# First expert's weights behind v, zero matmuls, five more PSUM banks and an eight-product last unit in an attention + mixture-of-experts kernel

## The chip, the cores and the metric

One core of one Trainium2 chip. The metric is the device time of one execution in microseconds (us), median of several runs. The kernel before takes 1044.17 us (three runs, 1044.15 to 1045.48). Differences are given as ratios with a 95% interval, and in us only where the trace shows where the us are. The engines by their names in the profile: PE (TensorE, matmuls; PEld is its weight load), DVE (VectorE) and ACT (ScalarE) for elementwise work, POOL (GpSimd, here the v casts and the weight transfers) and SP, which issues the k/q/v and output transfers.

## The reference

```python
# q, k, v: [8, 8, 576, 64]; w_gate [512, 8]; w1 [8, 512, 1024]; w2 [8, 1024, 512]
def _attn_ref(q, k, v):
    q_p, k_p = phi(q), phi(k)                      # phi(x) = x + 1 for x > 0, else exp(x)
    kv = einsum('bhsd,bhse->bhde', k_p, v); z = k_p.sum(2)
    return einsum('bhsd,bhde->bhse', q_p, kv) / (einsum('bhsd,bhd->bhs', q_p, z)[..., None] + 1e-6)

def _moe_ref(x, w_gate, w1, w2):                   # x: [4608, 512]
    P = exp(x @ w_gate - max)
    for _ in range(8):                             # row and column normalisation
        P /= P.sum(1, keepdims=True) + 1e-9
        P /= P.sum(0, keepdims=True) + 1e-9
        P *= N / E
    return sum(P[:, e:e+1] * (maximum(x @ w1[e], 0) @ w2[e]) for e in range(8))
```

## The kernel before

A small planner in Python (`_Plan`) decides the order of every instruction. Each task is given an engine (some may go to either of two, and the plan chooses), a guessed duration, a priority and for a transfer a guessed time to landing (`lat`). The planner runs a list schedule (whenever an engine is free, it takes the ready task of best priority) over these guesses and emits the instructions in that order. On the chip each engine works through its order strictly; semaphores, not the plan's clock, decide when. So a wrong guess makes no wrong result, but it can put an instruction that must wait in front of one that could run.

The work is 16 half batches of attention (`att`), then 8 experts of 9 units of 512 tokens: layer 1 (`hq`, 32 matmuls of 512 columns and 8 relus) and layer 2 (`ye`). Expert 0 uses the plain product, the others a seven-product scheme with sums S of h and T of w2 made on the vector engine. Matmul results go to PSUM banks (here four for ye, two for hq, two for attention); a matmul that needs a bank waits until DVE or ACT has copied out (evicted) what stands there. `acc` is the sum over the experts in SBUF.

```python
    def load_w(e, ten, nm, pl, ap, nk, prio, after=0.0, deps=()):
        g = S_.grp(pl)
        def fn(_):
            g["tile"] = wpool.tile([P, nk, DM * F // (nk * P)], FP16, tag=nm, name=nm)
            nc.gpsimd.dma_start(out=g["tile"], in_=AP(tensor=ten.tensor, offset=e * DM * F, ap=ap))
        t = add(("pool", 1.7), fn, acq=[g], prio=prio, lat=9.0, after=after, deps=deps)
        return g, t
    # ... att(b, g): one half batch, n = 2 * b + g
            tin[nm] = fadd(("sp", 1.05), fn, acq=[gr], prio=pr, lat=2.6)     # k, q, v: 576 KB each
    # ... exp and +1 on ACT or DVE, min and max on DVE, v cast on GpSimd (or DVE for n < 2)
        gkv, gz = [S_.grp(p_att), S_.grp(p_att)], S_.grp(p_kvz)              # p_att: two PSUM banks
    # ... two kv, two qt, den, three num, two xt: ten tiles, all from p_att
    w_t = {0: load_w1(0, prio=-300.0) + load_w2(0, prio=-250.0, after=4.0)}  # first thing in the program
    # ... expert 0: copy ye to acc, and when P is ready
                nc.vector.tensor_scalar(out=acc[g][:, tt, :], in0=acc[g][:, tt, :],
                                        scalar1=P_sb[:, gg, 0:1], scalar2=None, op0=ALU.mult)
            tf = add(("dve", 0.35), f_s, deps=[tf, p_done], prio=NG + g - 400.0)
    # ... combos(e): the four T of expert e from its w2
            last = add(("dve", 0.6), f_T, deps=[tw2, t_close, last], acq=..., prio=NG * e - 4.0)
    # ... expert e >= 2 is loaded when the buffers of expert e - 2 are free
```

The softmax here doesn't subtract the row's maximum and nothing guards it: scores larger than these inputs give would overflow.

Of the kernel before, what the change touches and what calls it, by code (L numbers as in the profile page):

```python
# [9 lines left out]
FP32 = mybir.dt.float32  # L10
# [106 lines left out]
def kernel(  # L117
# [61 lines left out]
    def load_w(e, ten, nm, pl, ap, nk, prio, after=0.0, deps=()):  # L179
        g = S_.grp(pl)  # L180

        def fn(_):
            g["tile"] = wpool.tile([P, nk, DM * F // (nk * P)], FP16, tag=nm, name=nm)
            nc.gpsimd.dma_start(out=g["tile"], in_=AP(tensor=ten.tensor, offset=e * DM * F, ap=ap))  # L184
        t = add(("pool", 1.7), fn, acq=[g], prio=prio, lat=9.0, after=after, deps=deps)
        return g, t

    def load_w1(e, **kw):
        return load_w(e, moe_w1, "w1", p_w1, [[F, P], [F * P, NDT], [1, F]], NDT, **kw)

    def load_w2(e, **kw):
        return load_w(e, moe_w2, "w2", p_w2, [[DM, P], [DM * P, NFT], [1, DM]], NFT, **kw)
# [10 lines left out]
    xt_done = {}  # L203

# [5 lines left out]
    def att(b, g):  # L210
        n = 2 * b + g
        pr = n - 100.0
        src = [[NJ * D, P], [2 * S * D, 2], [1, NJ * D]]
# [41 lines left out]
        tvv.append(fadd({"pool": 1.3, "dve": 0.75} if n < 2 else ("pool", 1.3), f_v, deps=[ta, tin["v"]],  # L255
                        use=[gvv, gin["v"]], prio=pr))
        gkv, gz = [S_.grp(p_att), S_.grp(p_att)], S_.grp(p_kvz)

        def f_kv(_):
            for hh in range(2):  # L260
                gkv[hh]["tile"] = aps.tile([P, 2, D + 1], FP32, tag="att", name=f"kv_ps{hh}")
# [60 lines left out]
        for i0, i1 in ((0, 2), (2, 4), (4, 5)):  # L322
            gn = S_.grp(p_att)

            def f_num(_, i0=i0, i1=i1, gn=gn):
                gn["tile"] = aps.tile([P, 2, 2, 2, D], FP32, tag="att", name="num_ps")
# [93 lines left out]
    w_t = {0: load_w1(0, prio=-300.0) + load_w2(0, prio=-250.0, after=4.0)}  # L420

    def f_init(_):
        make_identity(nc, ident)
        nc.gpsimd.dma_start(out=wg_sb, in_=AP(tensor=moe_w_gate.tensor, offset=0,
                                              ap=[[E, P], [E * P, NDT], [1, E]]))
    add(("pool", 1.5), f_init, prio=-290.0)
    for i in range(2):
        nc.vector.memset(vv_t[i][:, :, :, D], 1.0)
        nc.vector.memset(kvz_t[i], 0.0)
    for b in range(B):  # L430
        att(b, 0)
        att(b, 1)
        if b % 2 == 1:
            logits(b // 2)
    p_done = sinkhorn()
# [16 lines left out]
    def layer1(e, g):  # L452
# [10 lines left out]
        for f in range(NFT):  # L463
# [11 lines left out]
            t1 = add(("pe", 0.87), f_hq, deps=[tw1, prev_hq[0]] + xd, acq=[ghq], use=[gw1], prio=ui + 0.1 * f + 0.35)  # L475
# [12 lines left out]
    def unit0(g):  # L488
        e = 0
# [4 lines left out]
        for half in range(2):  # L494
            for tt in range(4):
                def f_y(_, half=half, tt=tt):
                    if half == 0:
                        gy[tt]["tile"] = yps.tile([P, 512], FP32, tag=f"ye{tt}", name=f"ye{tt}")
                    for f in range(4 * half, 4 * half + 4):
                        nc.tensor.matmul(gy[tt]["tile"], lhsT=gh["tile"][:, f, ds(P * tt, P)], rhs=gw2["tile"][:, f, :],  # L500
                                         start=(f == 0), stop=(f == NFT - 1))
                ty[tt] = add(("pe", 0.87), f_y, deps=[tw2, ty[tt]] + th[4 * half:4 * half + 4],
                             acq=[gy[tt]] if half == 0 else [], use=[gw2, gh],
                             prio=g + 0.1 * (4 * half + tt) + 0.3)
        for tt in range(4):
            def f_fin(eng, tt=tt):
                copy(eng, acc[g][:, tt, :], gy[tt]["tile"])

            def f_s(_, tt=tt):
                gg = 4 * g + tt  # L510
                nc.vector.tensor_scalar(out=acc[g][:, tt, :], in0=acc[g][:, tt, :],
                                        scalar1=P_sb[:, gg, 0:1], scalar2=None, op0=ALU.mult)
            tf = add({"act": 0.65, "dve": 0.69}, f_fin, deps=[ty[tt], t_close if g >= NA else None],
                     use=[gy[tt]], prio=g - 400.0)
            tf = add(("dve", 0.35), f_s, deps=[tf, p_done], prio=NG + g - 400.0)
            for dh in range(2):
                fin_prev[(4 * g + tt, dh)] = tf

    def combos(e):
# [3 lines left out]
        for i in range(4):  # L523
# [9 lines left out]
            last = add(("dve", 0.6), f_T, deps=[tw2, t_close, last], acq=[gT] if i == 0 else [], use=[gw2, gT],  # L533
# [3 lines left out]
    def unit(e, g, gT, tT):  # L537
# [18 lines left out]
        def sub(s):  # L556
# [14 lines left out]
            def pm(lhs, rhs, region, first, deps, acq, prio):  # L571
# [9 lines left out]
                return add(("pe", 0.44), f_m, deps=[tw2, tT] + deps, acq=[g_] if acq else [],  # L581
# [76 lines left out]
```

## Time and profile before

| | us |
|---|---|
| span of the profiled run | 1042.2 |
| TensorE (PE) busy | 1003.0 |
| first matmul of layer 1 | 39.67 |
| period of a unit of experts 1 to 7 | 13.02 |

Busy time includes matmuls at half clock. Lines of the timeline: start, length, engine, line, operation, in brackets the idle time before it and what ended it. This is GpSimd's row of the timeline around 210 us (start, length, engine, line, operation, in brackets the idle time before it and what ended it):

```profile
208.68 0.76 POOL L184 DMA_DIRECT2D w<-in_moe_w_dram  x1 [59.48 <-PE hq L470]
212.99 6.25 POOL L184 DMA_DIRECT2D w<-in_moe_w_dram  x1 [3.56 <-PE ye L500]
```

These are the issues of the third expert's w1 and w2. One normally takes 0.75 to 0.9 us; the second took 6.25. Over the same time DVE does the 36 scalings of acc by P, one every 0.40 us; here are the first 30, and the last one ends at 221.91 us:

```profile
206.57 12.19 DVE L511 TENSOR_SCALAR acc<-acc,P_sb 128x512 f32<-128x512 f32 x30
```

### The profile page before, as it was taken

What the parts mean: (1) busy time and instruction counts of PE and PEld (TensorE: products, weight loads), DVE (VectorE), ACT (ScalarE), POOL (GpSimd) and SP (SyncE); (2) the same over time, 40 slices, a digit from 0 to 9 for tenths busy, and PEclk for the clock granted to TensorE, in tenths of its full rate; (3) what the DMA queues carried; (4) which work ended last, traced back from release to release, by engine and by line L of the source; (5) the groups of instructions that cost most, each with busy time, mean ns of one, the idle gap of its engine ahead of it and who ended that gap; (6) DMA issues with size and microseconds to landing.
All of it is one profiled execution on the core that took longest, in us unless ns stands there. A gap on an engine that the chain in (4) does not pass through costs nothing.

```text
span 1042.2 us, 17323 instructions
## 1 busy us (share of the span) xinstructions
PE 1003.0 (96%) x7192; PEld 645.8 (62%) x7192; DVE 719.4 (69%) x1511; ACT 433.3 (42%) x717; POOL 42.2 (4%) x39
## 2 busy tenths in 40 slices
PE   2699999999999999999999999999999999999997
PEld 1455555456666666666666666666666666666664
DVE  4687775896666766676666766676666766666666
ACT  4677774443333333333333333333333333333331
POOL 2112110020000000000000000000000000000000
PEclk9999999999999999999999999999999999999999
DMA  9969510050004000050004000050004000013333
GB/s 272 309 189 271 168 47 2 1 81 1 1 1 66 17 1 1 1 81 2 1 1 66 16 1 2 1 82 1 1 2 66 16 2 1 1 41 81 81 82 82
DMA packets 31968, 55.66 MB, mean 53 GB/s; under 512 B 2704, under 2 KB 10896, under 8 KB 31888
## 3 DMA queue, kind: packets, MB, share of 16 engines
q1 hardware_dynamic: 18816, 37.76, 12.2%
q0 software_dynamic: 13072, 16.79, 10.1%
q8 instruction: 56, 0.92, 0.4%
q14 instruction: 24, 0.20, 0.1%
HBM read 61.88 MB, written 9.44 MB: 68 GB/s over the span
## 4 chain that ended last, share of the span: by engine, by line
PE 86%; issue 6%; DMA 4%; DVE 2%; ACT 0%; SPq 0%; POOL 0%; DVEq 0%; ACTq 0%; POOLq 0%
PE hq L470 44%; PE ye L579 36%; PE ye L500 3%; DMA vin<-in_v_dram 1%; DMA w<-in_moe_w_dram 1%; DMA qin<-in_q_dram 1%; PE kv_ps L265 1%; PE xt_ps L345 1%; PE qt_ps L291 1%; PE num_ps L329 1%; DVE acc L590 0%; DVE xn L334 0%; PE den_ps L306 0%; SPq L220 0%; DVE kvz L198 0%
## 5 line engine op out<-in xcount | busy, mean ns | idle before, releaser
L474 ACT ACTIVATE h<-hq 128x512 f16<-128x512 f32 x576 | 343.8, 597 | 548.5 <-PE hq L470 547.9
L470 PE MATMUL hq<-xT,w 128*128 128x512 f16 x2304 | 556.9, 379 | 0.0
L590 DVE SCALAR_TENSOR_TENSOR acc<-ye,P_sb,acc 128x256 f32<-128x256 f32 x882 | 396.3, 483 | 141.4 <-PE ye L579 141.4
L470 PEld LDWEIGHTS <-w 128*128 128x128 f16 x2304 | 223.2, 98 | 195.1 <-issue 0.3
L579 PEld LDWEIGHTS <-S 128*128 128x128 f16 x2016 | 196.8, 98 | 53.0 <-DVE S L553 3.7
L579 PE MATMUL ye<-T,S 128*128 128x256 f16 x1512 | 196.0, 273 | 2.4 <-DVE S L553 2.4
L579 PEld LDWEIGHTS <-h 128*128 128x128 f16 x1512 | 147.8, 98 | 58.6 <-issue 0.8
L553 DVE TENSOR_TENSOR S<-h 128x1024 f16<-128x1024 f16 x126 | 86.7, 688 | 112.5 <-ACT h L474 112.5
L579 PE MATMUL ye<-w,h 128*128 128x256 f16 x1008 | 130.8, 273 | 0.4 <-ACT h L474 0.4
L500 PE MATMUL ye<-w,h 128*128 128x512 f16 x288 | 69.8, 379 | 0.0
L579 PE MATMUL ye<-T,h 128*128 128x256 f16 x504 | 65.3, 273 | 0.3 <-DVE acc L590 0.2
L579 PE MATMUL ye<-w,S 128*128 128x256 f16 x504 | 65.3, 273 | 0.2 <-DVE S L553 0.2
L184 POOL DMA_DIRECT2D w<-in_moe_w_dram x16 | 19.1, 1193 | 638.8 <-PE hq L470 603.4
L553 DVE TENSOR_TENSOR S<-h,S 128x1024 f16<-128x1024 f16 x63 | 43.1, 684 | 0.0
L553 DVE TENSOR_TENSOR S<-S,h 128x1024 f16<-128x1024 f16 x63 | 42.9, 681 | 0.0
L500 PEld LDWEIGHTS <-h 128*128 128x128 f16 x288 | 26.1, 98 | 25.0
L334 DVE TENSOR_TENSOR xn<-num_ps,rden 128x512 f16<-128x512 f32 (+1 forms) x48 | 26.3, 595 | 2.8 <-PE num_ps L329 2.4
L200 POOL CAST vv<-vin 128x1152 f16<-128x1152 f32 x16 | 21.8, 1363 | 121.1 <-PE kv_ps L265 82.5
L229 ACT ACTIVATE ek<-kin 128x1152 f16<-128x1152 f32 x16 | 18.6, 1161 | 16.8 <-DMA kin<-in_k_dram 12.8
L265 PE MATMUL kv_ps<-vv,tk 64*128 64x130 f16 x288 | 12.3, 228 | 12.9 <-POOL vv L200 12.7
L198 DVE CAST kvz<-kv_ps 64x65 f16<-64x65 f32 x32 | 6.6, 222 | 22.1 <-ACT kvz L196 12.3
L291 PE MATMUL qt_ps<-ident,tq 128*128 128x128 f16 x144 | 14.6, 240 | 6.8 <-DVE kvz L198 4.6
(59 smaller groups left out, 329.5 us busy)
## 6 DMA issues: line engine op xcount, KB each, us to landing
w<-in_moe_w_dram POOLq DMA_DIRECT2D x16, 1024.0 KB, 9.6
kin<-in_k_dram SPq DMA_DIRECT2D x16, 576.0 KB, 5.2
qin<-in_q_dram SPq DMA_DIRECT2D x16, 576.0 KB, 4.9
vin<-in_v_dram SPq DMA_DIRECT2D x16, 576.0 KB, 6.1
out_dram<-acc SPq DMA_DIRECT2D x72, 128.0 KB, 2.4
wg_sb<-in_moe_w_gate_dram POOLq DMA_DIRECT2D x1, 8.0 KB, 15.3
```

Source lines behind the costliest of these rows:

```text
L184: nc.gpsimd.dma_start(out=g["tile"], in_=AP(tensor=ten.tensor, offset=e * DM * F, ap=ap))
L200: nc.gpsimd.tensor_copy(out=dst, in_=src)
L229: nc.scalar.activation(out=ge["tile"], in_=gin[nm]["tile"], func=AF.Exp)
L265: nc.tensor.matmul(gkv[hh]["tile"], lhsT=gt["k"]["tile"][s, j, :, :].rearrange("p r d -> p (r d)"), rhs=gvv["tile"][s, :, j, :], start=(j ...
L291: nc.tensor.transpose(gp["tile"][:, j - j0, :, :].rearrange("p h w -> p (h w)"), gt["q"]["tile"][:, j, :, :].rearrange("p r d -> p (r d)") ...
L334: nc.vector.tensor_tensor(out=gxn["tile"][:, i0:i1], in0=gn["tile"][:, 0:i1 - i0].rearrange("p i r h e -> p i (r h) e"), in1=grd["tile"][: ...
L470: nc.tensor.matmul(ghq["tile"], lhsT=gw1["tile"][:, c, ts(f, P)], rhs=xT[c][:, ds(512 * g, 512)], start=(c == 0), stop=(c == NDT - 1))
L474: nc.scalar.activation(out=gh["tile"][:, f, :], in_=ghq["tile"], func=AF.Relu)
L500: nc.tensor.matmul(gy[tt]["tile"], lhsT=gh["tile"][:, f, ds(P * tt, P)], rhs=gw2["tile"][:, f, :], start=(f == 0), stop=(f == NFT - 1))
L553: nc.vector.tensor_tensor(out=Sx[:, i], in0=a0, in1=a1, op=op)
L579: nc.tensor.matmul(g_["tile"][:, col, :], lhsT=lhs(kk), rhs=rhs(kk), start=(first and kk == 0), stop=(kk == 3), skip_group_check=True)
L590: nc.vector.scalar_tensor_tensor(out=dst, in0=g_["tile"][:, col, :], scalar=P_sb[:, gg, e:e + 1], in1=dst, op0=ALU.mult, op1=ALU.add)
```

## The change

Its intent: the attention of batch 0 should not share the DMA queues with the first expert's 4 MB of weights, PE should be warm and not held up by PSUM banks, and the last unit should not wait for sums S that nothing covers any more. Core of the diff (the merging of `unit0` into `unit_plain` cut):

```diff
-    def load_w(e, ten, nm, pl, ap, nk, prio, after=0.0, deps=()):
+    def load_w(ten, nm, pl, ap, cut, e, prio, parts=1, after=0.0, deps=(), lats=(9.0,)):
...    (each of `parts` DMAs: columns of w1 or row blocks of w2, plan ("pool", 1.1), lat=lats[i])
-    w_t = {0: load_w1(0, prio=-300.0) + load_w2(0, prio=-250.0, after=4.0)}
+    w_t = {0: load_w1(0, prio=-290.0, parts=2, deps=[vcast[0]], lats=(5.0, 7.0))
+           + load_w2(0, prio=-280.0, parts=2, deps=[vcast[1]], lats=(7.0, 9.0))}
+    add(("pool", 0.8), f_wg, prio=-270.0, deps=[w_t[0][3][1]])
+        def ps_home(kind, i):
+            if n < 2 and kind == "kv":
+                return p_hq, hqp, "hq"
+            if n < 2 and kind == "num":
+                return p_ye[i], yps, f"ye{i}"
+            return p_att, aps, "att"
-        tvv.append(fadd({"pool": 1.3, "dve": 0.75} if n < 2 else ("pool", 1.3), f_v, deps=[ta, tin["v"]],
+        tvv.append(fadd(("pool", 1.3), f_v, deps=[ta, tin["v"]],
+    def f_warm(_):
+        nc.tensor.matmul(yw[0], lhsT=warm[:, 0:P], rhs=warm, start=True, stop=True)
+    for i in range(34):
+        twa = add(("pe", 0.3), f_warm, deps=[twa], use=[gyw], prio=900.0, after=1.2 + 0.5 * i)
-            if e == 0:
-                unit0(g)
+            if e == 0 or (e == E - 1 and g == NG - 1):
+                unit_plain(e, g)
```

More of the change, by code (lines that the diff above doesn't have):

```diff
@@ L177, with f_al, fn @@
     p_ye = [S_.pool(1) for _ in range(4)]
-    def load_w(e, ten, nm, pl, ap, nk, prio, after=0.0, deps=()):
+    def load_w(ten, nm, pl, ap, cut, e, prio, parts=1, after=0.0, deps=(), lats=(9.0,)):
         g = S_.grp(pl)
-        def fn(_):
-            g["tile"] = wpool.tile([P, nk, DM * F // (nk * P)], FP16, tag=nm, name=nm)
-            nc.gpsimd.dma_start(out=g["tile"], in_=AP(tensor=ten.tensor, offset=e * DM * F, ap=ap))
-        t = add(("pool", 1.7), fn, acq=[g], prio=prio, lat=9.0, after=after, deps=deps)
-        return g, t
+        ts_ = []
+        def f_al(_):
+            g["tile"] = wpool.tile([P, ap[1][1], ap[2][1]], FP16, tag=nm, name=nm)
+        tal = add(("none", 0.0), f_al, acq=[g], prio=prio, after=after, deps=deps)
+        for i in range(parts):
+            def fn(_, i=i):
+                dst, a, off = g["tile"], [list(x) for x in ap], e * DM * F
+                if parts > 1:
+                    n = a[cut][1] // parts
+                    off += i * n * a[cut][0]
+                    a[cut][1] = n
+                    dst = dst[:, i * n:(i + 1) * n, :] if cut == 1 else dst[:, :, i * n:(i + 1) * n]
+                nc.gpsimd.dma_start(out=dst, in_=AP(tensor=ten.tensor, offset=off, ap=a))
+            ts_.append(add(("pool", 1.1), fn, use=[g], prio=prio, lat=lats[i], deps=[tal]))
+        return g, [ts_[0], ts_[-1]]
     def load_w1(e, **kw):
-        return load_w(e, moe_w1, "w1", p_w1, [[F, P], [F * P, NDT], [1, F]], NDT, **kw)
+        return load_w(moe_w1, "w1", p_w1, [[F, P], [F * P, NDT], [1, F]], 2, e, **kw)
     def load_w2(e, **kw):
-        return load_w(e, moe_w2, "w2", p_w2, [[DM, P], [DM * P, NFT], [1, DM]], NFT, **kw)
+        return load_w(moe_w2, "w2", p_w2, [[DM, P], [DM * P, NFT], [1, DM]], 1, e, **kw)
     def copy(e, dst, src):
@@ L203 @@
     xt_done = {}
+    vcast = {}
     def fadd(*a, **kw):
@@ L254, in f_v @@
             copy(e, gvv["tile"][:, :, :, 0:D], gin["v"]["tile"])
-        tvv.append(fadd({"pool": 1.3, "dve": 0.75} if n < 2 else ("pool", 1.3), f_v, deps=[ta, tin["v"]],
+        tvv.append(fadd(("pool", 1.3), f_v, deps=[ta, tin["v"]],
                         use=[gvv, gin["v"]], prio=pr))
-        gkv, gz = [S_.grp(p_att), S_.grp(p_att)], S_.grp(p_kvz)
+        vcast[n] = tvv[0]
+        hkv = ps_home("kv", 0)
+        gkv, gz = [S_.grp(hkv[0]), S_.grp(hkv[0])], S_.grp(p_kvz)
         def f_kv(_):
             for hh in range(2):
-                gkv[hh]["tile"] = aps.tile([P, 2, D + 1], FP32, tag="att", name=f"kv_ps{hh}")
+                gkv[hh]["tile"] = hkv[1].tile([P, 2, D + 1], FP32, tag=hkv[2], name=f"kv_ps{hh}")
             for j in range(NJ):
@@ L322, in att, with f_num @@
         for i0, i1 in ((0, 2), (2, 4), (4, 5)):
-            gn = S_.grp(p_att)
-            def f_num(_, i0=i0, i1=i1, gn=gn):
-                gn["tile"] = aps.tile([P, 2, 2, 2, D], FP32, tag="att", name="num_ps")
+            hn = ps_home("num", i0 // 2)
+            gn = S_.grp(hn[0])
+            def f_num(_, i0=i0, i1=i1, gn=gn, hn=hn):
+                gn["tile"] = hn[1].tile([P, 2, 2, 2, D], FP32, tag=hn[2], name="num_ps")
                 for i in range(i0, i1):
@@ L419, with f_wg @@
     nc.vector.memset(ones_t, 1.0)
-    w_t = {0: load_w1(0, prio=-300.0) + load_w2(0, prio=-250.0, after=4.0)}
+    warm = const.tile([P, 512], FP16, tag="warm", name="warm")
+    nc.vector.memset(warm, 0.0)
     def f_init(_):
         make_identity(nc, ident)
+    def f_wg(_):
         nc.gpsimd.dma_start(out=wg_sb, in_=AP(tensor=moe_w_gate.tensor, offset=0,
@@ L426, with f_wa @@
     add(("pool", 1.5), f_init, prio=-290.0)
+    def f_warm(_):
+        nc.tensor.matmul(yw[0], lhsT=warm[:, 0:P], rhs=warm, start=True, stop=True)
+    gyw = S_.grp(p_ye[3])
+    yw = []
+    def f_wa(_):
+        yw.append(yps.tile([P, 512], FP32, tag="ye3", name="yw"))
+    twa = add(("none", 0.0), f_wa, acq=[gyw], prio=-300.0)
+    for i in range(34):
+        twa = add(("pe", 0.3), f_warm, deps=[twa], use=[gyw], prio=900.0, after=1.2 + 0.5 * i)
     for i in range(2):
@@ L474, in f_rl @@
                 nc.scalar.activation(out=gh["tile"][:, f, :], in_=ghq["tile"], func=AF.Relu)
-            t1 = add(("pe", 0.87), f_hq, deps=[tw1, prev_hq[0]] + xd, acq=[ghq], use=[gw1], prio=ui + 0.1 * f + 0.35)
+            t1 = add(("pe", 0.87), f_hq, deps=[tw1[f // 4], prev_hq[0]] + xd, acq=[ghq], use=[gw1], prio=ui + 0.1 * f + 0.35)
             prev_hq[0] = t1
@@ L486, in out_dma, with unit_plain @@
         add(("sp", 1.0), f_o, deps=deps, prio=0.0)
-    def unit0(g):
-        e = 0
+    def unit_plain(e, g):
         gw1, tw1, gw2, tw2 = w_t[e]
@@ L501, in f_y, with f_fin, f_s @@
                                          start=(f == 0), stop=(f == NFT - 1))
-                ty[tt] = add(("pe", 0.87), f_y, deps=[tw2, ty[tt]] + th[4 * half:4 * half + 4],
+                ty[tt] = add(("pe", 0.87), f_y, deps=[tw2[half], ty[tt]] + th[4 * half:4 * half + 4],
                              acq=[gy[tt]] if half == 0 else [], use=[gw2, gh],
-                             prio=g + 0.1 * (4 * half + tt) + 0.3)
+                             prio=e * NG + g + 0.1 * (4 * half + tt) + 0.3)
         for tt in range(4):
-            def f_fin(eng, tt=tt):
-                copy(eng, acc[g][:, tt, :], gy[tt]["tile"])
-            def f_s(_, tt=tt):
-                gg = 4 * g + tt
+            gg = 4 * g + tt
+            def f_fin(eng, tt=tt, gg=gg):
+                if e == 0:
+                    copy(eng, acc[g][:, tt, :], gy[tt]["tile"])
+                else:
+                    nc.vector.scalar_tensor_tensor(out=acc[g][:, tt, :], in0=gy[tt]["tile"],
+                                                   scalar=P_sb[:, gg, e:e + 1], in1=acc[g][:, tt, :],
+                                                   op0=ALU.mult, op1=ALU.add)
+            def f_s(_, tt=tt, gg=gg):
                 nc.vector.tensor_scalar(out=acc[g][:, tt, :], in0=acc[g][:, tt, :],
                                         scalar1=P_sb[:, gg, 0:1], scalar2=None, op0=ALU.mult)
-            tf = add({"act": 0.65, "dve": 0.69}, f_fin, deps=[ty[tt], t_close if g >= NA else None],
-                     use=[gy[tt]], prio=g - 400.0)
-            tf = add(("dve", 0.35), f_s, deps=[tf, p_done], prio=NG + g - 400.0)
-            for dh in range(2):
-                fin_prev[(4 * g + tt, dh)] = tf
+            if e == 0:
+                tf = add({"act": 0.65, "dve": 0.69}, f_fin, deps=[ty[tt], t_close if g >= NA else None],
+                         use=[gy[tt]], prio=g - 400.0)
+                tf = add(("dve", 0.35), f_s, deps=[tf, p_done], prio=NG + g - 400.0)
+                for dh in range(2):
+                    fin_prev[(gg, dh)] = tf
+            else:
+                tf = add(("dve", 0.75), f_fin, deps=[ty[tt], p_done, fin_prev[(gg, 0)], fin_prev[(gg, 1)]],
+                         use=[gy[tt]], prio=e * NG + g - 400.0)
+                out_dma(g, tt, [tf])
     def combos(e):
@@ L532, in f_T @@
                 nc.vector.tensor_tensor(out=T[:, i], in0=a0, in1=a1, op=op)
-            last = add(("dve", 0.6), f_T, deps=[tw2, t_close, last], acq=[gT] if i == 0 else [], use=[gw2, gT],
+            last = add(("dve", 0.6), f_T, deps=tw2 + [t_close, last], acq=[gT] if i == 0 else [], use=[gw2, gT],
                        prio=NG * e - 4.0)
@@ L580, in f_m @@
                                          start=(first and kk == 0), stop=(kk == 3), skip_group_check=True)
-                return add(("pe", 0.44), f_m, deps=[tw2, tT] + deps, acq=[g_] if acq else [],
+                return add(("pe", 0.44), f_m, deps=tw2 + [tT] + deps, acq=[g_] if acq else [],
                            use=[gw2, gT, gh, gS, g_], prio=ui + 0.3 + prio + 0.02 * s)
@@ L618 @@
         if e >= 2:
-            w_t[e] = load_w1(e, prio=float(e), deps=[w_t[e - 1][1]]) + load_w2(e, prio=float(e), deps=[w_t[e - 1][3]])
+            w_t[e] = load_w1(e, prio=float(e), deps=w_t[e - 1][1][1:]) + load_w2(e, prio=float(e), deps=w_t[e - 1][3][1:])
         if e > 0:
```

## The prediction

> **What bounds the kernel now.** I read the page first, its row of slices:
>
> ```profile
> PE   2699999999999999999999999999999999999997
> ...
> PEclk9999999999999999999999999999999999999999
> DMA  9969510050004000050004000050004000013333
> ```
>
> One slice is 26 us. TensorE (PE) is full from the third slice to the last but one. Only the first two slices, where the DMA row shows 9, and the last one have room. I then took the windows view, whose columns are stretch, length, busy time of PE, PEld, DVE, ACT and POOL with counts, granted clock, DMA share, GB/s:
>
> ```profile
> 10.00:15.00 5.00, 1.16 (x18) 0.89 (x17) 0.04 (x1) 0.00 (x0) 1.15 (x1) 1.00 1.12 291
> 35.00:40.00 5.00, 3.48 (x26) 2.75 (x26) 4.32 (x9) 3.73 (x5) 0.00 (x0) 1.00 1.05 390
> 40.00:45.00 5.00, 5.00 (x50) 2.60 (x49) 2.37 (x5) 3.04 (x9) 1.15 (x1) 1.00 0.76 218
> 45.00:50.00 5.00, 3.05 (x26) 1.81 (x25) 4.24 (x10) 3.40 (x5) 0.00 (x0) 1.00 0.81 236
> 220.00:230.00 10.00, 8.61 (x61) 5.63 (x59) 8.81 (x20) 2.90 (x6) 0.00 (x0) 1.00 0.72 104
> 1028.57:1036.50 7.93, 6.09 (x49) 4.10 (x46) 7.01 (x15) 0.60 (x1) 0.00 (x0) 1.00 0.23 52
> 1036.50:1042.20 5.70, 0.01 (x1) 0.00 (x0) 0.53 (x2) 0.00 (x0) 0.00 (x0) 0.83 0.67 156
> ```
>
> PE idles 1042.2 - 1003.0 = 39.2 us. By stretch: 26.65 before 40 us (40 less the eight busy figures there, 13.35), 1.95 in 40 to 50, 1.7 from 50 to 220, 1.39 in 220 to 230, 1.84 in the last unit and 5.69 after the last matmul. Between 230 and 1028 us it is dense: the chain repeats every 13.02 us per unit, which is 32 matmuls of 512 columns and 56 of 256 without a gap. The change leaves that stretch alone, so it can win only at the two ends.
>
> What holds up the first 40 us stands in the chain of waits, cut to the start:
>
> ```profile
> 3.46 15.24 DMA vin<-in_v_dram
> ...
> 20.38 12.49 DMA qin<-in_q_dram
> ...
> 32.90 0.76 DVE tq L235
> 33.66 0.03 issue
> 33.69 0.19 DVE rden L312
> ...
> 39.88 1.04 PE hq L470 x4
> ```
>
> A v load takes 15.2 us and then a q load 12.5. After them the reciprocal of the second half batch (rden) comes late only because DVE has the q cast of a later half batch ahead of it in its order. Layer 1 (hq) cannot start before batch 0, two half batches, is done: 39.67 us in the timeline. The waits of the first 40 us name the beginning:
>
> ```profile
> POOL vv L200 <- DMA vin<-in_v_dram: 15.9, 3, 7.2
> PE kv_ps L265 <- POOL vv L200: 12.7, 1, 12.7
> ```
>
> **What the Trainium skill says.** "DMA: Bandwidth & Descriptors", section SWDGE vs HWDGE vs iDMA: software-made and hardware-made descriptors feed different queues inside each engine, served round-robin, and a cast must be issued by GpSimd. The packet records agree: from 18 to 20 us the weight queue moved 181 packets and the k/q/v queue 182. A 576 KB load landed every 1.5 us alone (30 to 38 us) and every 2.96 us beside w2 (18 to 27 us). "TensorE: Matmul & The Clock Gate", Part 1: a PE left idle about 3.4 us falls to half clock. The PEclk row does not show it (1.00 throughout), but the work does:
>
> ```profile
> 12.66 1.16 PE L265 MATMUL kv_ps<-vv,tk 64*128 64x130 f16 x18 [12.66 <-POOL vv L200]
> ...
> 51.80 0.69 PE L265 MATMUL kv_ps<-vv,tk 64*128 64x130 f16 x18
> ```
>
> The same page, section Architectural detail: DVE and ACT are strictly first in, first out; rden behind a foreign q cast agrees. "PSUM — Partial Sum Buffer", Specifications: eight banks per partition. The kernel has assigned them all: four ye, two hq, two for attention. The six others are empty in the first 39 us, while ten tiles of every half batch take turns on two.
>
> **The change part by part.**
>
> *Weights behind v.* In before the weight issues start at 1.24 and 3.42 us; w1's packets landed 5.4 to 14.2 us, those of w_gate to 17.5, w2's 16.5 to 28.7. The first six loads landed at 4.0, 5.8, 10.6, 14.2, 15.9 and 18.0 us. The two behind q0 have most of w1's packets beside them. Without weights, at 1.5 us each, they become about 4.0, 5.6, 7.1, 8.6, 10.1 and 11.6. The first v cast starts 0.8 us after landing and takes 1.15, so kv runs at about 9.0 instead of 12.66, and the sixth load is in 6.4 us sooner. GpSimd issues w1 behind that first cast, at 9.0. In before 3.5 to 4 us went by from the issue to the first packets, so about 12.5 here. Halving w1 by columns turns 512 packets of 2 KB into 1024 of 1 KB, like w2's, of which 1024 took 12.2 us. Hence halves of 6 us: w1 at 18.5 and 24.5, w2 at 30.5 and 36.5. The later k/q/v loads now share the queue: k2 13, q2 16, v2 19, k3 22, q3 25, v3 28. This does not make DMA traffic less; it moves the attention of batch 0 ahead of the weights.
>
> *Free banks.* For the first two half batches kv goes to hq banks and num to ye banks. That takes five of ten tiles off the two attention banks. In the timeline the second kv matmul ran at 27.75, although its v cast ended at 19.90: 7.8 us lost to banks and orders of engines. With 1.15 for the cast from v1's landing at 11.6 plus 0.8, kv1 can run at 13.5. From its kv (27.75) to its last xT copy (39.25) before needed 11.5 us, of which the rden wait on q3 (landed 31.9) is a few. I take 9 to 11: batch 0 is done at 22.5 to 24.5 if its DVE steps stand only behind loads of half batch 2 (19 us), and at 27 if behind q3 (25). I choose 24.5 for the first hq. w1's first half is there at 18.5. Its second serves hq 5 to 8, from 28 us; w2 serves ye, 8 x 0.86 = 6.9 us of hq plus attention later, 32 us and on. Both just suffice.
>
> *Gain at the front.* 39.67 - 24.5 = 15.2 us. Off that: before had already done nine more transposes by then (0.5 us). Its half batches up to the sixth had nearly all been loaded, whereas in after PE will meet its orders with loads still late (v3 at 28, w2 at 36.5, the plan counts on earlier). I charge 4 us for such stalls, against the 1.95 us in 40 to 50 that before pays. Net: 15.2 - 0.5 - (4 - 1.95) = about 12.5 us.
>
> *Zero matmuls.* 34 of 512 columns: 34 x 0.216 = 7.3 us warm, 14.5 at half clock, all planned within the first 18 us, where PE has 26.65 us of idling. They buy warm attention matmuls: kv 1.16 becomes 0.69, nine or ten transposes 1.3 become about 0.7. That is 1 to 2 us on the chain of batch 0, part of which comes back as a zero matmul standing in front of a ready one (0.2 to 0.4 each). It is inside the 9 to 11 above; I add nothing.
>
> *Last unit.* Seven products cost 56 x 0.109 = 6.1 us, eight (32 matmuls of 512 columns x 0.216) 6.9: +0.8. In before PE ran from the last unit's first product at 1028.41 to 1036.50, 8.1 us, of which 2.0 are waits on the S sums of DVE:
>
> ```profile
> 1032.21 1.05 PE L579 MATMUL ye<-T,S 128*128 128x256 f16 x8 [1.18 <-DVE S L553]
> ```
>
> Those go; one wait for the last relu (0.6) may stay. PE ends 0.6 to 1.2 us sooner. The end behind it is bound by eight issues on SP:
>
> ```profile
> 1034.57 4.96 SPq L485 DMA_DIRECT2D out_dram<-acc  x8
> ```
>
> They cost 0.62 each and end 3.0 us after PE. With tiles finishing every 0.86 us and a 512-wide eviction of about 0.75, the first issue comes about 1.8 before PE's end and the last ends 3.2 after. So 0.2 goes back: gain 0.7 us.
>
> Sum: 12.5 + 0.7 = 13.2 us off 1044.17, so 1031.
>
> **The rivals.** *The orders eat it.* The program's orders come from a plan that counts a load at 1.05 us; on the chip it is 1.5 to 3. For it: the 12.5 us q load of the chain. Against: fewer banks to wait for puts batch 0 further ahead in the orders. If rden of the second half batch stands behind q3 again, hq starts at 27 to 30 and the gain is 7 to 9: 1035 to 1037. *Late weights become the bound.* w_gate comes last, 512 packets of 16 B that took 4.4 us even in before, and the first logits could hold PE some us; so could w2. That gives 2 to 4 us back: about 1034. *Everything runs to schedule.* hq starts at 21, no extra stalls: the gain is 18 to 19 and the result 1025. More is hardly possible: two half batches need their six loads (11.6) and then the chain of the second. *DMA total as the bound*: to 40 us before had loaded 18 tiles and all weights; that is time PE spends well if batch 0 comes first, so I don't believe in no gain at all.
>
> **Range and chances.** Front gain from 6 to 18 us with the tail's 0.7 gives 1025 to 1038. Over 2% means below 1023.3, or 21 us: nearly the whole 26.65 plus 1.95, though the first loads alone forbid 9 of it: 4%. Slower by 2% would need a new wait in the dense part, which the change does not touch: 1%.
>
> **What would show each step.** The first vv cast at about 7.9 and kv at 9.0 us; the second kv near 13.5; w1's halves landing near 18 and 24; the first hq of w near 24.5; PE idle before 40 us down from 26.65 to 12 to 16, the zero matmuls not counted as work; kv x18 near 0.7 in the first 15 us. At the end no S wait in the last unit, and PE ending within 6 us of the span's end. It is wrong if hq starts after 31, if PE shows new waits of over 5 us between 25 and 60 us, or if the 13.02 us rhythm changes.

## More of the kernel before

The scaling of expert 0 by P comes late, since the routing P is ready only when all attention is done.

## The result, and the profile after

The changed kernel takes 1047.66 us (median of four, 1046.31 to 1048.04) beside 1044.80 for the one before: ratio 1.0025, interval 1.0008 to 1.0042. A ratio is the mean time of one kernel's fast runs over that of the other's of the same rounds, so not quite the ratio of the medians that I quote. I had said 1031 and a range of 1025 to 1038.

The profiled run has a span of 1044.5 us, 2.3 more than before. Where they come from is read by following the same matmul through both traces:

| matmul of layer 1 | before, us | after, us | difference |
|---|---|---|---|
| first | 39.7 | 31.4 | -8.2 |
| 17th | 44.6 | 43.0 | -1.5 |
| 289th (first of expert 1) | 208.2 | 206.2 | -2.0 |
| 353rd | 234.2 | 238.0 | +3.9 |
| 2001st | 906.0 | 909.9 | +3.9 |
| end of the span | 1042.2 | 1044.5 | +2.3 |

So the front won 2.0 us, 5.9 were lost between 206 and 238 us, and the end won 1.6. From 238 us on the difference stays at 3.9: the 13.02 us rhythm is untouched. Up to the 289th matmul a row of this table counts layer 1 alone, and the two kernels put different pieces of attention between its matmuls. So I also counted all of PE's work done by a given time, every matmul at its full-clock time (0.216 us for 512 columns, by the trace before), zero matmuls left out: the kernel after leads by 3.2 us at 40 and at 50 us and by 1.8 at 200 us. So of the 8.2 us by which layer 1 starts sooner 3.2 are left at 40 us.

**The front.** The windows view of the kernel after (columns as in the prediction):

```profile
10.00:15.00 5.00, 5.00 (x58) 3.50 (x59) 4.85 (x11) 4.40 (x6) 3.96 (x5) 0.67 1.07 376
35.00:40.00 5.00, 1.12 (x9) 0.56 (x7) 1.29 (x3) 0.97 (x1) 0.70 (x1) 1.00 1.19 328
40.00:45.00 5.00, 4.27 (x20) 2.14 (x20) 1.83 (x4) 4.27 (x7) 0.00 (x0) 0.66 1.04 387
```

At 10 to 15 us PE is full (zero matmuls and half clock included), where before it did 1.16 us. But at 35 to 40 it does 1.12 us instead of 3.48, and all other engines starve as well while the DMA share is 1.19. The chain of waits says on what:

```profile
3.73 9.21 DMA vin<-in_v_dram
...
14.17 11.50 DMA vin<-in_v_dram
...
27.77 11.23 DMA qin<-in_q_dram
39.01 0.02 issue
39.03 1.16 ACT eq L247
40.19 0.49 ACT h L512
40.69 0.04 issue
40.73 1.87 PE hq L508 x4
```

It is the same figure as before, further on. Layer 1 has begun, and its second relu (h) stands on ACT behind the exponential of a q that lands only at 38.1 us. The timeline of ACT shows both places where that happens:

```profile
28.64 1.16 ACT L247 ACTIVATE eq<-qin 128x1152 f16<-128x1152 f32 x1 [2.56 <-DMA qin<-in_q_dram]
29.71 0.62 ACT L206 COPY xT<-xt_ps 128x576 f16<-128x576 f16 x1
...
39.03 1.16 ACT L247 ACTIVATE eq<-qin 128x1152 f16<-128x1152 f32 x1 [5.07 <-DMA qin<-in_q_dram]
40.10 1.06 ACT L512 ACTIVATE h<-hq 128x512 f16<-128x512 f32 x2
```

The last xT copy of batch 0, which frees layer 1, waits from 26.6 to 29.7 behind load 12 (q of the fourth half batch, called q3, its last packet at 27.3); two relus wait until 40.1 behind load 16 (q4, 38.1). The waits of PE that follow are 3.5 and 4.6 us:

```profile
30.38 1.13 PE L285 MATMUL kv_ps<-vv,tk 64*128 64x130 f16 x17 [3.46 <-ACT xT L206]
40.73 1.87 PE L508 MATMUL hq<-xT,w 128*128 128x512 f16 x4 [4.61 <-ACT h L512]
```

Behind each of them matmuls run at half clock (granted 0.62 in 30 to 35 us, 0.66 in 40 to 45).

**The zero matmuls** all ran, but in this run the first 13 did not warm PE:

```profile
1.33 5.51 PE L453 MATMUL yw<-warm 128*128 128x512 f16 x13 [1.33 <-DVE warm L442]
9.93 1.16 PE L285 MATMUL kv_ps<-vv,tk 64*128 64x130 f16 x18 [3.09 <-POOL vv L210]
```

Thirteen took 0.42 us each throughout, and the first kv behind them 1.16, as cold as before. The second kv, at 14.87 us, took 0.69.

**The middle.** GpSimd's and DVE's rows of the timeline after:

```profile
202.85 13.95 DVE L554 TENSOR_SCALAR acc<-acc,P_sb 128x512 f32<-128x512 f32 x35
206.69 11.29 POOL L194 DMA_DIRECT2D w<-in_moe_w_dram  x2 [60.39 <-PE hq L508]
```

```profile
230.41 0.69 DVE L580 TENSOR_TENSOR T<-w 128x1024 f16<-128x1024 f16 x1 [7.05 <-DMA w<-in_moe_w_dram]
231.02 1.65 DVE L638 SCALAR_TENSOR_TENSOR acc<-ye,P_sb,acc 128x256 f32<-128x256 f32 x4
232.33 1.87 PE L627 MATMUL ye<-T,h 128*128 128x256 f16 x8 [6.03 <-DVE acc L638]
```

The first issue alone took 10.41 us, until 217.1, when the row of 35 scalings (202.85 to 216.80) had ended. w2 landed at 230 us. DVE stood 7.05 us before T of the third expert, which is not needed before that expert starts (its first layer-1 matmul is at 329 us). Evictions of layer 2 stood behind it, and PE behind them; two rows of the windows view, the second at a granted clock of 0.74:

```profile
220.00:230.00 10.00, 6.31 (x43) 3.98 (x41) 3.36 (x7) 2.39 (x4) 0.00 (x0) 0.92 1.09 187
230.00:240.00 10.00, 7.67 (x42) 4.65 (x42) 7.07 (x15) 2.39 (x4) 0.00 (x0) 0.74 0.00 0
```

Before, the same 220 to 230 us had 8.61 busy and 230 to 240 had 10.00. The 5.9 us are about the sum: 6.0 of wait, 1.4 of half clock in the twelve matmuls behind it (1.87 + 1.62 us, where the trace shows 1.04 + 1.03 at full clock), less the 1.4 that the kernel before idles there.

**The end.** The last unit's layer 2 and the output issues, timeline after:

```profile
1034.84 3.83 PE L537 MATMUL ye<-w,h 128*128 128x512 f16 x16
...
1036.90 4.95 SPq L523 DMA_DIRECT2D out_dram<-acc  x8
```

No wait for S is left. PE ends at 1038.69, 1.7 us sooner against the lag of 3.9; the issues end 3.2 us behind PE, as the prediction worked out (before: 3.0).

### The profile page after: what moved, and what is told of

Read it like the earlier page. It is cut to its first block, busy times and chain, and to the rows that moved or that the text cites. A ratio compares the mean times of both kernels' runs of the same rounds, so it can differ in the third digit from the quotient of the medians.

```text
span 1044.5 us, 17330 instructions
## 1 busy us (share of the span) xinstructions
PE 1013.9 (97%) x7202; PEld 646.2 (62%) x7202; DVE 713.3 (68%) x1495; ACT 435.8 (42%) x720; POOL 46.9 (4%) x41
## 4 chain that ended last, share of the span: by engine, by line
PE 85%; issue 7%; DMA 4%; DVE 2%; POOL 1%; ACT 0%; SPq 0%; POOLq 0%; DVEq 0%; ACTq 0%
PE hq L508 43%; PE ye L627 36%; PE ye L537 4%; DMA vin<-in_v_dram 2%; DMA w<-in_moe_w_dram 1%; DMA qin<-in_q_dram 1%; PE kv_ps L285 1%; PE xt_ps L366 1%; PE num_ps L350 0%; PE qt_ps L311 0%; POOL w L194 0%; DVE kvz L208 0%; SPq L238 0%; DVE tk L260 0%; POOL vv L210 0%
## 5 line engine op out<-in xcount | busy, mean ns | idle before, releaser
L638 DVE SCALAR_TENSOR_TENSOR acc<-ye,P_sb,acc 128x256 f32<-128x256 f32 x868 | 390.6, 483 | 141.0 <-PE ye L627 140.9
L627 PEld LDWEIGHTS <-S 128*128 128x128 f16 x1984 | 194.1, 98 | 48.9
L627 PE MATMUL ye<-T,S 128*128 128x256 f16 x1488 | 192.8, 273 | 0.0
L627 PE MATMUL ye<-w,h 128*128 128x256 f16 x992 | 128.6, 273 | 0.0
L537 PE MATMUL ye<-w,h 128*128 128x512 f16 x320 | 77.6, 379 | 0.0
L194 POOL DMA_DIRECT2D w<-in_moe_w_dram x18 | 24.9, 1387 | 640.4 <-PE hq L508 609.5
L247 ACT ACTIVATE eq<-qin 128x1152 f16<-128x1152 f32 x16 | 18.6, 1162 | 8.7 <-DMA qin<-in_q_dram 8.3
L206 ACT COPY acc<-ye 128x512 f32<-128x512 f32 x26 | 15.2, 585 | 9.3 <-PE ye L537 8.9
```

The source lines that it names most:

```text
L194: nc.gpsimd.dma_start(out=dst, in_=AP(tensor=ten.tensor, offset=off, ap=a))
L206: nc.scalar.copy(out=dst, in_=src)
L247: nc.scalar.activation(out=ge["tile"], in_=gin[nm]["tile"], func=AF.Exp)
L537: nc.tensor.matmul(gy[tt]["tile"], lhsT=gh["tile"][:, f, ds(P * tt, P)], rhs=gw2["tile"][:, f, :], start=(f == 0), stop=(f == NFT - 1))
L627: nc.tensor.matmul(g_["tile"][:, col, :], lhsT=lhs(kk), rhs=rhs(kk), start=(first and kk == 0), stop=(kk == 3), skip_group_check=True)
L638: nc.vector.scalar_tensor_tensor(out=dst, in0=g_["tile"][:, col, :], scalar=P_sb[:, gg, e:e + 1], in1=dst, op0=ALU.mult, op1=ALU.add)
```

## The experiments

Fifteen kernels, in four groups (e, f, g with f6, h), four or five runs of each; every group ran on another chip. Each ratio is to the kernel before in the same rounds on the same chip (seven to nine runs), so a comparison across groups, such as g4 with f1 or h1 with g4, is one of ratios.

| run | what | median us | ratio (95%) |
|---|---|---|---|
| e1_tlate | after, T later | 1039.41 | 0.9947 (0.9934 to 0.9959) |
| e2_scale_act | after, scalings on ACT | 1039.11 | 0.9945 (0.9932 to 0.9959) |
| e3_b_tlate | before, T later | 1044.52 | 0.9996 (0.9983 to 1.0008) |
| e4_b_eight | before, eight products | 1043.17 | 0.9984 (0.9971 to 0.9996) |
| f1_truelat | e1, true landings in the plan | 1032.77 | 0.9884 (0.9869 to 0.9900) |
| f2_now2 | e1, first w2 not read | 1032.25 | 0.9879 (0.9865 to 0.9892) |
| f4_nowarm | e1, no zero matmuls | 1039.34 | 0.9948 (0.9935 to 0.9960) |
| f5_nobanks | e1, two banks | 1043.86 | 0.9990 (0.9977 to 1.0002) |
| f6_wearly | e1, weights at the start | 1038.11 | 0.9940 (0.9926 to 0.9953) |
| g1_b_truelat | e3, true landings | 1035.81 | 0.9914 (0.9900 to 0.9927) |
| g3_w1late | f1, second expert later | 1032.04 | 0.9882 (0.9868 to 0.9895) |
| g4_nowarm | f1, no zero matmuls | 1031.22 | 0.9872 (0.9859 to 0.9886) |
| h1_wearly_true | g4, weights at the start | 1035.35 | 0.9915 (0.9900 to 0.9929) |
| h2_truelat_only | after, true landings | 1034.08 | 0.9897 (0.9883 to 0.9912) |
| h3_nobanks | g4, two banks | 1032.41 | 0.9888 (0.9871 to 0.9904) |

### The middle: T, scalings and descriptors

My theory after the traces: the 5.9 us in the middle are T in DVE's order, waiting for weights whose descriptors GpSimd could not write while DVE ran its scalings. The rival: DVE's backlog itself holds PE, T is an onlooker.

**e1_tlate.**
```diff
-            last = add(("dve", 0.6), f_T, deps=tw2 + [t_close, last], ...
+            last = add(("dve", 0.6), f_T, deps=tw2 + [t_close, last, hq_at[(e - 1, 5)] if e >= 2 else None], ...
```
(`hq_at[(e, g)]` is the last layer-1 task of a unit.)

> The changed kernel, with one thing more: the four DVE sums T that the third expert needs from its second-layer weights (and those of the later experts) are tied in the plan to layer 1 of a late unit of the expert before, so that they stand some 60 us later in DVE's order. Theory (the loss after 206 us is DVE, in order, standing 7.05 us before a T whose weights came late, though nobody needs that T for another 100 us): the 6.0 us PE wait near 226 to 232 us and the cold matmuls behind it go; the changed kernel was 2.0 us ahead of the one before at the end of the first expert and fell to 3.9 behind, so 5.9 us come back: 1047.4 - 5.9 = about 1041.5, ratio to the kernel before 0.997. Rival (DVE's burst of 36 scalings itself makes PE wait, T is an onlooker): the wait stays or turns up under another name, time stays within 1.5 us of 1047.

It gave 8 us. The wait is gone; the windows view of this run in the stretch where before had 8.61 and after 6.31:

```profile
220.00:230.00 10.00, 10.00 (x70) 6.58 (x68) 7.09 (x15) 3.07 (x6) 0.00 (x0) 1.00 1.10 186
```

Yet its weight issue took 10.41 us as well. So the late landing does no harm by itself; T's place in the order makes it a stall. It gained more than the 5.9 us I expected, 7.4 us between the two profiled runs: 5.9 for the stall, and 1.6 because it now passes this stretch faster than the kernel before, whose 1.39 us of idling there are gone too.

**e2_scale_act.**
```diff
-                nc.vector.tensor_scalar(out=acc[g][:, tt, :], in0=acc[g][:, tt, :],
-                                        scalar1=P_sb[:, gg, 0:1], scalar2=None, op0=ALU.mult)
+                nc.scalar.activation(out=acc[g][:, tt, :], in_=acc[g][:, tt, :], func=AF.Copy, scale=P_sb[:, gg, 0:1])
-            tf = add(("dve", 0.35), f_s, ...
+            tf = add(("act", 0.62), f_s, ...
```

> The changed kernel with the 36 scalings of acc by P moved from DVE to ACT (36 x about 0.6 us, planned there). Theory (those 512-wide SBUF to SBUF DVE operations keep GpSimd from writing the descriptors of the third expert's weights: issue of 10.4 us): the two weight issues near 205 us take 0.7 to 0.9 us each, w2's packets end 8 to 12 us sooner than 230 us, T does not wait and PE's 6.0 us wait goes: about 1041.5 to 1043. Rival (the issue is long because of GpSimd's own wait or of the DMA queue): the issues stay at 6 to 10 us, time stays.

The issues without the burst on DVE, GpSimd's timeline of this run:

```profile
208.11 0.75 POOL L194 DMA_DIRECT2D w<-in_moe_w_dram  x1 [60.36 <-PE hq L508]
212.64 0.89 POOL L194 DMA_DIRECT2D w<-in_moe_w_dram  x1 [3.77 <-PE ye L537]
```

T stays where the change has it and no longer waits; the time is that of e1. Both links are shown: the DVE scalings stretch the issue, T's place turns that into PE time. The Trainium skill has the first link ("SBUF — State Buffer", section SBUF: two separate sides): a DVE operation in a two-port mode locks GpSimd out, so that it "cannot write the descriptors". That these scalings run in such a mode no run here shows directly; the issue times with and without them are what is shown. I had not read it for this change, because the change adds no such operation.

**e3_b_tlate** (the same edit on the kernel before):

> The kernel before with the same later T. Theory: it has the same trap, but only 1.2 us of it (its w1 issue slipped through in 0.76 us), so it gains 0.5 to 1.5 us: ratio 0.9985 to 0.9995; the front and the end of the change are then worth e1 against e3, 2.5 to 3.5 us. Rival (T late costs something in the dense stretch): ratio over 1.000.

Nothing measurable (0.9996). Before has the trap, but its first issue slipped in between two scalings (0.76 us), so DVE waited only 1.2 us before T. PE's idling there (1.39 us) is mostly another wait, 1.2 us for an S that stands behind the last six scalings, and e3 keeps it. A change that moved this region by only 2 us turned DVE's 1.2 us before T into 7.

**e4_b_eight** (`unit_plain` for the last unit of the kernel before, nothing else):

> The kernel before with the last unit in eight products and nothing else of the change. From the traces (6.4 us more lag at the last layer-1 matmul would be the reordered unit; at the end of the span the lag fell from 3.9 to 2.3): the part alone is worth 1.6 us, ratio 0.9985. My prediction had 0.7 (ratio 0.9993). Rival (the SP issues of the output bound the end and nothing is won): ratio 1.000.

0.9984, 1.6 us, as the trace said (the profiled run is 0.6 behind at the 2001st layer-1 matmul and 0.9 ahead at the end). Predicted were 0.7; the interval, 0.4 to 3.0 us, does not exclude that, the traces put it at 1.5 to 1.6.

### The front: orders or bytes

**f1_truelat**, on e1:
```diff
-            tin[nm] = fadd(("sp", 1.05), fn, acq=[gr], prio=pr, lat=2.6)
+            slow = 2 < n < 5 or (n == 2 and nm != "k")
+            tin[nm] = fadd(("sp", 2.95 if slow else 1.5), fn, acq=[gr], prio=pr, lat=3.2)
-    ... lats=(5.0, 7.0)) ... lats=(7.0, 9.0))
+    ... lats=(9.6, 14.5)) ... lats=(17.3, 21.7))
```

> The later-T kernel (1039.41 us, ratio 0.9947), its plan fed with the landings that the changed kernel's trace shows: 1.5 us per k/q/v load, 2.95 for the eight loads beside the weights, 9.6 to 21.7 us for the weight halves of the first expert. Nothing else changes; only the orders of the engines do. Theory A (orders: PE's 3.2 and 4.4 us waits come from ACT standing before loads 15 and 16, which the plan thought landed): those two waits go, PE does 3 to 8 us more work by 45 us, the time falls to 1032 to 1037, ratio 0.988 to 0.993. Theory B (DMA total: batch 1 cannot be done before loads up to the twelfth, 27 us, and w2 up to 37 have landed, in whatever order): the waits only move, time 1038 to 1041, ratio 0.994 to 0.997.

Theory A held: the bytes are the same, the first, second and so on to the sixteenth load land within 0.3 us of where they did in the kernel after, and 6.6 us are gone. But the plan orders the loads and chooses engines too. In the kernel after, v3 went before q3 and two v before q4; here q3 is the eleventh load (24.2 us, there 27.3) and q4 the fourteenth (32.9, there 38.1), the very two that ACT stood behind. ACT ran 709 instructions against 720, DVE 1506 against 1495. So "orders" means the order of instructions, the order of loads and the choice of engine together; no run splits them. The windows view, against 1.12 in 35 to 40 us above:

```profile
25.00:30.00 5.00, 4.98 (x33) 2.30 (x31) 2.74 (x7) 3.25 (x5) 1.15 (x1) 0.66 1.13 294
30.00:35.00 5.00, 5.00 (x40) 2.84 (x38) 4.34 (x10) 3.98 (x6) 0.00 (x0) 1.00 1.14 297
35.00:40.00 5.00, 5.00 (x54) 2.79 (x53) 4.04 (x11) 1.93 (x4) 2.17 (x2) 1.00 1.06 364
```

and its timeline:

```profile
24.98 3.53 PE L510 MATMUL hq<-xT,w 128*128 128x512 f16 x8
```

Layer 1 starts at 25.0 us; I had predicted 24.5.

**f2_now2** (zeros for the first expert's w2, 2 MB less to read; its result is wrong by 35%):

> Wrong on purpose: the later-T kernel with zeros in place of the first expert's second-layer weights, so that 2 MB less are read in the first 40 us and the orders stay (two DVE memsets of about 0.6 us come in). Theory B (DMA total): loads 12 to 16 land 3 to 6 us sooner and all of it reaches PE, ratio 0.989 to 0.991. Theory A (orders): the waits for loads 15 and 16 shrink by the same landings, so this run alone does not tell A from B; but if it gains under 2 us (ratio over 0.993), DMA traffic is not the bound at all.

The sixteenth load landed at 32.4 instead of 38, and 7.1 us were gained. As expected in advance, this alone does not tell orders from bytes: a stale order gets better when its loads come sooner (q4 lands here at 32.4, in f1 at 32.9). Together with f1 it says that the front was limited by the mismatch of the two, and could be mended from either side.

**g1_b_truelat** (the kernel before with T later and its own landings in its plan: per k/q/v load 1.5 to 4.8 us, w1 12.7, w2 23.2):

> The kernel before (weights at the start, no zero matmuls, two banks, seven products), with the later T and with its plan fed with its own landings (v0 10.6 us, k1 14.2, v1 18.0, w1 14.2, w2 28.7). Theory (the change's own front parts need true orders to pay, and true orders alone do part of it): 2 to 5 us faster than before, ratio 0.995 to 0.998, first hq near 34 to 38. Rival 1 (the plan's false landings were the whole trouble, the weights' place does not matter): 7 us or more, ratio under 0.9935. Rival 2 (in before the two banks and v's landing bind, orders do not): ratio over 0.9985.

0.9914, 9 us, first layer-1 matmul at 28.5: Rival 1 by its number. (The later T alone, e3, gave nothing measurable.) Without any part of the change, true landings in the plan alone start layer 1 sooner (28.5) than the change does with false ones (31.4). In the kernel before, as in the change, false landings were the larger trouble.

### The parts of the front

**f6_wearly** (e1 with whole weights at the start and the old figures):

> The later-T kernel (ratio 0.9947) with the weights of the first expert whole and at the start again, as before the change, plan figures of before; banks, zero matmuls and eight products stay. Theory (loading behind v is what lets batch 0 run early, worth 1 to 3 us under the stale plan): ratio 0.9955 to 0.9975, first kv at 12.7 us. Rival (the place of the weights is neutral, DMA moves the same in 37 us): ratio 0.9940 to 0.9953.

0.9940 against 0.9947: neutral. Under false landings, loading behind v brings nothing.

**h1_wearly_true** (the same question with true landings, against g4):

> As the kernel with true landings and without zero matmuls (1031.22 us, ratio 0.9872), but the first expert's weights whole and at the start, the plan fed with the landings of the kernel before. If the weights' place is neutral (DMA moves the same bytes by 37 us): ratio 0.986 to 0.9885. If loading behind v is worth the 3 to 4 us by which v0 lands earlier: ratio 0.9895 to 0.992.

0.9915 against 0.9872, intervals apart: 4 us. That it is the early landing that pays is not shown: counted in PE work as above, h1 is only 0.7 us behind g4 at 60 us (9.7 against 10.4 ahead of the kernel before), and 3.1 at 80 us (5.9 against 9.0). Most of the difference comes from what the two plans do between 60 and 80 us, long after the first expert's weights are in.

**f5_nobanks** (`n < 2` to `n < 0` in `ps_home`, on e1) and **h3_nobanks** (the same on g4):

> The later-T kernel with kv and num of the first two half batches back on the two attention banks. Theory (the bank share of the front's 3.5 us is real but batch 0 then waits for loads anyway): 0 to 2 us slower, ratio 0.9947 to 0.9966. Rival (banks are what lets batch 0 run ahead): 3 us or more slower, ratio over 0.9975, hq after 35 us.

> As the kernel with true landings and without zero matmuls (ratio 0.9872), with kv and num of the first two half batches on the two attention banks again. Under the stale plan the banks were worth 4.5 us. If that was mostly the order that the plan made of them: 0 to 1.5 us here, ratio 0.987 to 0.9887. If the banks themselves hold batch 0 up: 3 us or more, ratio over 0.990.

4.5 us under false landings (0.9990), where ACT's orders now wait 11.9 us in all for q loads and hq for xT 5.7. With true landings 0.9888 against 0.9872, with overlapping intervals: 1.7 us, not told from nothing. The banks' worth was mostly what order the plan made of them.

**f4_nowarm** (`range(34)` to `range(0)` on e1) and **g4_nowarm** (the same on f1):

> The later-T kernel without the 34 zero matmuls. My prediction gave them 1 to 2 us inside the chain of batch 0; the landings after 25 us, which bind later, would hide that. Theory (hidden): kv and transposes of the first 15 us are cold again (1.16 us), hq starts within 1 us of 31.2, ratio 0.994 to 0.996. Rival (the clock matters): 2 us or more slower, ratio over 0.9965.

> The kernel with true landings without the 34 zero matmuls. There hq starts at 25.0 us straight behind batch 0, so a colder chain is not hidden by a late load any more. If the clock is worth the 1 to 2 us of my prediction: ratio 0.9895 to 0.9905, hq at 26 to 27. If DVE, not PE, paces batch 0 (as its chain of waits shows): ratio 0.988 to 0.989, hq at 25.

Without the zero matmuls the time is the same in e1 (0.9948) and no worse in f1 (0.9872 against 0.9884, in different rounds). In the profiled run of f1 they did warm PE (17 zero matmuls in 5.43 us, first kv 0.69), in g4 layer 1 starts 1.5 us later. In PE work f1 is 2.8 us ahead of g4 at 40 us, and 0.4 behind at 240: what they bring early is gone later. They buy nothing in the whole time.

**g3_w1late** (`after=60.0`, `after=70.0` to 100 and 110 for the second expert, on f1):

> The kernel with true landings (1032.77 us, ratio 0.9884), the second expert's weights asked for at 100 and 110 us of the plan in place of 60 and 70, so that they do not share the queue with k/q/v between 48 and 78 us. If those transfers cause the loss there (its lead over before fell from 14 to 9 us of PE work between 60 and 80 us), 2 to 5 us more: ratio 0.984 to 0.987. If the in-order DVE chain of attention causes it whatever the loads do: ratio 0.987 to 0.990.

0.9882, no difference from f1: the second expert's loads are not the main thing that makes f1 lose lead behind 60 us (in PE work 14.0 us at 60 us and 9.6 at 80; g3 has 14.2 and 11.1). The chain of waits there runs through DVE's attention steps in their order; I did not test that further.

**h2_truelat_only** (after, with true landings and T where the change has it):

> The changed kernel with true landings in its plan and nothing else (T stays early in DVE's order, zero matmuls stay). If the stall near 226 us belongs to T's place alone: it stays, and the gain is the front's 6.6 us of 1047.4: about 1041, ratio 0.996 to 0.998. If the shifted front moves the third expert's weight issues off the DVE burst: no stall over 2 us and 1033 to 1035, ratio 0.989 to 0.991.

0.9897, 1034 us: my first theory there fell. The stall did not come back (T waited 1.6 us): in this run the first weight issue slipped in, the second took 6.25, as in before:

```profile
200.78 0.75 POOL L194 DMA_DIRECT2D w<-in_moe_w_dram  x1 [58.60 <-PE hq L509]
205.09 6.25 POOL L194 DMA_DIRECT2D w<-in_moe_w_dram  x1 [3.56 <-PE ye L538]
```

T's early place is needed for the stall, but the first issue being shut out is needed too, and that hangs on where the issue falls in the burst. I did not try to steer that, but the traces agree on it. In all 16 that have the scalings on DVE, an issue that began 0.12 or 0.13 us after the start of a scaling got in (ten of them, 0.75 or 0.76 us, the next scaling 0.7 instead of 0.48), and one that began 0.24 to 0.27 us after it was shut out (ten second issues, six first ones). All that were shut out ended 0.3 to 0.5 us after the row of scalings, when DVE had turned to evictions that read PSUM.

The fastest right version is g4: true landings, T later, no zero matmuls, 1031.22 us, faster than both kernels (ratio to before 0.9872, and the kernel after was at 1.0025); the intervals of f1, g3 and h3 overlap its own. That it comes out at the 1031 which I had predicted for another kernel is chance.

## Why the prediction was wrong, point by point

1. **Bound of the kernel before:** right for 238 us to the last unit, where nothing moved. Wrong in that only the two ends could change (point 5).
2. **When transfers land:** nearly right. Last packets: v0 7.4 us (7.1 predicted), the sixth load 11.9 (11.6), w1's halves 19.8 and 25.5 (18.5 and 24.5), w2's 31.2 and 36.8 on 15 of the 16 DMA engines (30.5 and 36.5). The first cast came at 8.48 (7.9), kv at 9.93 (9.0), the second kv at 14.87 (13.5). One was wrong in kind: I had q3 at 25 before v3 at 28; the plan issued v3 first, at 24.4, and q3 landed at 27.3.
3. **First hq at 24.5:** this is the step of the front that failed. I wrote "batch 0 is done at 22.5 to 24.5 if its DVE steps stand only behind loads of half batch 2 (19 us), and at 27 if behind q3 (25). I choose 24.5". It was the other case, on ACT: xT stood behind q3, landed 27.3, then copied by 30.3, and hq came at 31.4, later than the 27 to 30 of that case because q3 itself was late. My own sign "it is wrong if hq starts after 31" was met; the one of new waits over 5 us between 25 and 60 us was not (4.6). f1 shows that 24.5 was the right figure for an order that knows the landings (25.0).
4. **"I charge 4 us for such stalls":** too small. From 31.4 us, where both kernels had done the same work before their first hq and the lead was 8.2 us, it fell to 3.2 us of PE work by 40 us, with a wait of 4.6 us behind load 16 and half clock. I had said that PE's idling before 40 us would go from 26.65 to 12 to 16 us, zero matmuls not counted as work; the trace has 25.6 (f1: 17.0). I counted the earlier start of hq as gain, minus a flat charge, instead of asking which loads ACT and DVE would meet before each relu. Net 2.0 us instead of 12.5. f1 recovers 6.6 of the difference.
5. **A new wait in the middle:** not in the prediction at all. It said "Slower by 2% would need a new wait in the dense part, which the change does not touch", and listed 1.39 us of idling at 220 to 230 us without asking for its cause. It was a wait for S behind the scalings (1.2 us), and the row of scalings is half of the trap that the change fell into: 5.9 us in the trace, 8 us in e1 and e2 with what before loses there. Where the burst falls against the weight issue is luck, which nothing in the prediction could have told; that T stands there early was in the plan.
6. **Zero matmuls, 1 to 2 us "inside the 9 to 11":** not there (f4, g4).
7. **Free banks:** part of the front's sum without a figure of their own; 4.5 us under false landings, 1.7 and not told from nothing with true ones.
8. **Last unit, 0.7 us:** right in kind, 1.6 in size (e4). The issues end 3.2 us behind PE as worked out; the term that was mis-sized is PE's end, 1.7 us sooner instead of 0.6 to 1.2, since the wait for the last relu that I left in (0.6) is not there (PE is busy 9.83 of the last 9.90 us). My 2.0 us of "waits on the S sums" was all of PE's idling in that unit; the waits view gives 1.3 to S and 0.4 to a relu.
9. **Rivals:** "The orders eat it" was the right one and I gave it 7 to 9 us of gain. With the wait in the middle nothing was left.

The sum: -2.0 + 5.9 - 1.6 = +2.3 us of span, which is what was measured. What stays open: what takes back part of the lead of f1, h1, h2 and g3 between 60 and 80 us (3 to 5 us of PE work; g1, g4 and h3 lose 0 to 1.5), how much of f1's gain is the order of the loads, and why an issue gets in at 0.12 us after the start of a scaling and not at 0.25.

## What to carry to other kernels

When engines follow an order fixed in advance, feed the plan the landing times of the trace before moving any transfer; here that alone gave the old kernel 9 us, and without it the move gave 2. Before predicting a shift of the start, look in the dense part for instructions that wait early for something needed late (a wait of 1.2 us before T was in the profile): any shift can make such a wait longer. Count an earlier start as gain only up to the next load that some engine must meet in its order.

## What the Trainium skill lacked or had wrong

- "SBUF — State Buffer", section SBUF: two separate sides, tells of one DVE operation that blocks GpSimd's descriptors. None of its text says that a row of short ones can shut an issue out for the rest of the row: 10.41 us, some 26 scalings of 0.40 us, while the same issue in the kernel before took 0.76 us; nor that an issue begun 0.12 us after the start of a scaling gets in and one begun 0.25 us after it does not (16 traces). Moving the scalings to ACT brought both issues to 0.75 and 0.89 us.
- No page that I found says how a fixed order meets late transfers, which was the largest effect here: 6.6 us in f1 and 9 us in g1, from the plan's landing figures alone.
